# A state-space scan and a feed-forward network on one core: halves of a chunk's tokens, and another order and another engine for the lead-in's loads

## The chip, the cores and the metric

The kernel runs on one core of a Trainium2 chip. The core has five engines that each take their instructions in order: TensorE (PE in the profile; its weight loads are PEld), VectorE (DVE), ScalarE (ACT), GpSimd (POOL) and SyncE (SP). Data moves between DRAM and the core's memory through 16 DMA engines; SP and ACT can issue such transfers, each into a queue of its own. The metric is the time of one execution on the device in microseconds (us).

## The reference

Inputs are `x` (4 batches, 8 heads, 768 tokens, 32 channels), a decay `a` per batch, head and token, and `B` and `C` with 16 states per token. A linear recurrence runs over the tokens of each batch and head. In blocks of tokens it reads:

```python
la = log(clip(a)); cum = cumsum(la)             # within a block
M = (C @ B.T) * exp(cum[i] - cum[j]) * (i >= j)
y = M @ x + (C @ state) * exp(cum)
state = exp(sum(la)) * state + sum_j exp(cum[-1] - cum[j]) * B[j] x[j]
```

The outputs of the 8 heads of a token are put side by side to 256 numbers, and a feed-forward network follows for the 3072 tokens: `leaky_relu(y @ w_in, 0.01) @ w_out` with 2048 hidden features. All is float32 in the reference; the weights reach the kernel as 64-bit floats and are decoded on the chip.

## The kernel before, in words

The kernel takes 96 tokens to a chunk (8 chunks) and a chunk of one batch to a unit (32 units, `u = 4 * chunk + batch`). For each unit PE computes the score products (L288 or L365), DVE multiplies them with a tile of decays `lt` (L293 or L374), and `unit_products` multiplies the result with the tokens (L305) and the states' inputs `bn` with the same tokens (L314). The tile `xs` of a chunk holds the tokens of all 4 batches in its first 96 partitions and the states that enter the chunk in the last 16. `unit_halves` copies the new states on ACT (L336) and puts them on POOL into the next chunk's `xs` (L339), then takes the outputs as a high part `xh` (ACT, L341) and a low part `xl` (DVE, L344).

The decays of the first two units come directly from the logarithms (`reach`, L172, L215). Those of units 2 to 15 come from row sums of the logarithms: `split_sums` makes them on PE (L194) and splits them in three 16-bit parts on DVE (L195 to L198), which a DMA writes to DRAM (`parts_d`, L561), and two DMAs per group of units bring them back in another layout, into `dr` (L224) and `dl` (L227). One short matmul pair per unit (L234) then gives the exponents, and ACT the exp (L242). The first such pair of DMAs fetches the rows of units 2 to 5, later ones two units each.

The loop over units 0 to 15 is the lead-in. In it PE runs one unit's scores, the unit before's products and the decay of the unit after, DVE decodes the first weight blocks in steps (`decode`, L390 to L428), and `ps_d`, two PSUM buffers of two banks, holds in turn a unit's outputs and another unit's decay. `state_decay` (L269, POOL) scales a chunk's `bn` once it has landed.

Then the feed-forward network runs as 94 steps of one block of 128 features for 512 tokens: six matmuls in (L486), the leaky relu on ACT (L493, L496), the rest on DVE (L499), six matmuls out (L510). Units 16 to 31 are worked in between, two at a time.

The order of all instructions is written out by hand, and each engine keeps it (`manual_schedule`). Waits are put in from the data that instructions share. The loads come from helper functions (`fetch_w` L82, `fetch_bc` L86, `fetch_bn` L90, `fetch_x` L96) and before the change every DMA of the lead-in is issued by SP, so SP's order is: `la`, `bc` and `xs` of chunk 0, `parts_d`, `bn` of chunk 0, the first weight block, the rows `dr` and `dl`, and then `bc`, `bn`, `xs` of chunk 1, the second weight block and `xs` of chunk 2.

Of the kernel before, what the change touches and what calls it, by code (L numbers as in the profile page):

```python
# [10 lines left out]
F32 = mybir.dt.float32  # L11
# [6 lines left out]
NB, NH, S, D, N = 4, 8, 768, 32, 16  # L18
Q = 96
NC = S // Q  # L20
QE = Q + N
DM = NH * D
# [4 lines left out]
TS = 512  # L27
# [28 lines left out]
def scan_ffn(ctx: ExitStack, tc: tile.TileContext, a_l, bc_l, bn_l, x_l, w_l, out_l):  # L56
# [4 lines left out]
    wst = ctx.enter_context(tc.tile_pool(name="wst", bufs=3))  # L61
    wr = ctx.enter_context(tc.tile_pool(name="wr", bufs=RAWS))
    pbc = ctx.enter_context(tc.tile_pool(name="pbc", bufs=2))
    pxs = ctx.enter_context(tc.tile_pool(name="pxs", bufs=3))
    plt = ctx.enter_context(tc.tile_pool(name="plt", bufs=4))
    px = ctx.enter_context(tc.tile_pool(name="px", bufs=4))
    pg = ctx.enter_context(tc.tile_pool(name="pg", bufs=LAG + 1))
# [12 lines left out]
    def fetch_w(f, eng=nc.sync):  # L80
        raws[f] = wr.tile([128, 2 * DM, 2], U32, name="raw")
        eng.dma_start(raws[f].rearrange("p c w -> p (c w)"), w_l[f].bitcast(U32))  # L82

    def fetch_bc(c, eng=nc.sync):
        bcs[c] = pbc.tile([128, BC_COLS], F32, name="bc")
        eng.dma_start(bcs[c], bc_l[c])  # L86

    def fetch_bn(c):
        bns[c] = pbc.tile([QE, NB * NH * N + N], F32, name="bn")
        nc.sync.dma_start(bns[c], bn_l[c])  # L90

    def alloc_x(c):
        xss[c] = pxs.tile([QE, NB, DM], F32, name="xs")

    def fetch_x(c, eng=nc.sync):
        eng.dma_start(xss[c][:Q].rearrange("p b c -> p (b c)"), x_l[c])  # L96


    idle = const.tile([128, 512], BF16, name="idle")
# [13 lines left out]
    fetch_bc(0)  # L113
    for c in range(3):
        alloc_x(c)
    fetch_x(0)


    upto = const.tile([Q, QE], F32, name="upto")
# [97 lines left out]
                start=False, stop=True,  # L217
            )

    def decay_rows_of(u, n):  # L220
        p, b = u * NH, (u - DIRECT) % SLOTS
        r = Q + 3 * NH
        rows = parts_d[p:p + n * NH]
        nc.sync.dma_start(  # L224
            dr[r:r + 3, b:b + n].rearrange("i b h q -> i (b h) q"), rows.rearrange("p i q -> i p q")
        )
        nc.sync.dma_start(  # L227
            dl[Q:r, b:b + n, :Q], rows.rearrange("(b h) i q -> (h i) b q", h=NH)
        )

    def decay_pe(u, space):
        b = (u - DIRECT) % SLOTS
        for g in range(2):
            nc.tensor.matmul(  # L234
                heads_of(space, g), lhsT=dl[:KD, b], rhs=dr[:KD, b, 4 * g:4 * g + 4],
                start=True, stop=True,
            )
        decay_of(u, space)

    def decay_of(u, space):  # L240
        lt = lts[u] = plt.tile([QE, NH, Q], F32, name="lt")
        nc.scalar.activation(  # L242
            lt.rearrange("p (g h) i -> p g (h i)", g=2), space[:QE, :, :4 * Q], AF.Exp
        )
# [33 lines left out]
    def scores(u, warm=0):  # L278
        c, b = divmod(u, NB)
        spread = bcs[c][:, B_COLS:].rearrange("p (b i) -> p b i", b=NB)  # L280
        lt = lts[u].rearrange("p (g h) i -> p g (h i)", h=2)
        for half in range(2):
            sc = score_tile()
            if half == 0 and warm:
                keep_warm(sc[:, 0], warm)
            for g in range(2):
                r = 32 * (2 * half + g)
                nc.tensor.matmul(  # L288
                    sc[:QE, g, :2 * Q], lhsT=bcs[c][r:r + 32, b * QE:(b + 1) * QE],
                    rhs=spread[r:r + 32, b], start=True, stop=True,  # L290
                )
            heads = lt[:, 2 * half:2 * half + 2]
            nc.vector.tensor_tensor(out=heads, in0=sc[:QE, :, :2 * Q], in1=heads, op=ALU.mult)  # L293
# [3 lines left out]
    def unit_products(u, space, off=0):  # L297

        c, b = divmod(u, NB)
        kk = QE if c else Q  # L300
        mt, xs = lts[u], xss[c][:, b]
        for g in range(2):
            for hh in range(4):
                h = 4 * g + hh
                nc.tensor.matmul(  # L305
                    space[hh * D:(hh + 1) * D, g, off:off + Q],
                    lhsT=xs[:kk, h * D:(h + 1) * D], rhs=mt[:kk, h, :], start=True, stop=True,
                )
        if c + 1 < NC:

            for h in range(NH):
                hh = h % 4
                n0 = (b * NH + h) * N
                nc.tensor.matmul(  # L314
                    space[hh * D:(hh + 1) * D, h // 4, off + Q:off + Q + D],
                    lhsT=bns[c][:kk, n0:n0 + 2 * N],
                    rhs=xs[:kk, h * D:(h + 1) * D], start=True, stop=True,
                )

    def unit_halves(u, space, off=0):  # L320

        c, b = divmod(u, NB)
        yp = space[:, :, off:off + Q]
        pieces = []
        i = 0
        while i < Q:
            t, col = divmod(u * Q + i, TS)
            n = min(Q - i, TS - col)
            if col == 0:
                xh[t] = px.tile([128, 2, TS], F32R, name="xh")  # L330
                xl[t] = px.tile([128, 2, TS], F32R, name="xl")
            pieces.append((t, slice(col, col + n), slice(i, i + n)))
            i += n
        if c + 1 < NC:
            stage = pst.tile([128, 2, D], F32, name="stage")
            nc.scalar.copy(stage, space[:, :, off + Q:off + Q + D])  # L336
            to = xss[c + 1][Q:QE, b].rearrange("n (g h d) -> n g h d", g=2, d=D)
            for hh in range(4):
                nc.gpsimd.tensor_copy(to[:, :, hh], stage[hh * D:hh * D + N])  # L339
        for t, to, of in pieces:  # L340
            nc.scalar.copy(xh[t][:, :, to], yp[:, :, of])  # L341
        def rest():
            for t, to, of in pieces:
                nc.vector.tensor_tensor(  # L344
                    out=xl[t][:, :, to], in0=yp[:, :, of], in1=xh[t][:, :, to], op=ALU.subtract
                )
        return rest

    def unit_out(u, space):
        unit_products(u, space)  # L350
        return unit_halves(u, space)
# [183 lines left out]
                nc.sync.dma_start(out_l[m, :, t * TS:(t + 1) * TS], ob)  # L535


    with tc.tile_pool(name="ps_d", bufs=2, space=PSUM, reuse_waits="tile") as ps_d:

        def free_tile():  # L540
            return ps_d.tile([128, 2, TS], F32, name="pd")

        nc.vector.tensor_scalar(
            out=la, in0=la, scalar1=1e-6, scalar2=1.0, op0=ALU.max, op1=ALU.min,
        )
        nc.scalar.activation(la, la, AF.Ln)
        nc.vector.tensor_copy(dl[:Q], upto_b.unsqueeze(1).to_broadcast([Q, SLOTS, QE]))
        fill_later(0, 2)
        pds = [free_tile() for _ in range(DIRECT)]
        for u in range(DIRECT):  # L550
            fill_reach(u)
        for u in range(DIRECT):
            decay_mask(pds[u])
        split_sums(first[:, 0, :Q])
        fill_less(0, nc.scalar.copy)
        fill_less(1, nc.scalar.copy)
        second = score_tile()
        keep_warm(second[:, 1], WARM2)
        columns(erev, after, AF.Exp, second[:, 0])
        fill_later(2, SLOTS)  # L560
        nc.sync.dma_start(parts_d, parts)  # L561
        fetch_bn(0)
        fetch_w(0)
        decay_rows_of(DIRECT, SLOTS)
        fetch_bc(1)
        fetch_bn(1)
        fetch_x(1)
        fetch_w(1)
        fetch_x(2)
        decay_direct(0, pds[0])  # L570
        decay_of(0, pds[0])
        scores(0)
        state_decay(0)
        for b in range(2, SLOTS):
            fill_less(b, nc.gpsimd.tensor_copy)
        decay_direct(1, pds[1])
        decay_of(1, pds[1])
        decode_abs(0)
        for u in range(PE_DECAY):
            if u + 1 < PE_DECAY:  # L580
                scores(u + 1, 2 if u < 2 else 1)
            if u == 11:
                alloc_x(4)
            rest = unit_out(u, free_tile())
            v = u + 2
            if v < PE_DECAY:
                decay_pe(v, free_tile())
                if v % 2 and v + SLOTS <= PE_DECAY:
                    decay_rows_of(v + SLOTS - 1, 2)
            rest()  # L590
            if u > 2:
                settle()
            if u == 0:
                decode(2)
            elif u != 3:
                decode(1)
            if u == 2:
                state_decay(1)


            if u in (2, 6):
                fetch_bc(u // 4 + 2)
            if u in (3, 7):
                fetch_bn(u // 4 + 2)
                fetch_w(u // 4 + 2)
            if u == 3:
                alloc_x(3)
                fetch_x(3)
            if u in (6, 10):
                state_decay((u + 2) // 4)  # L610
        settle()
        decode(1)
# [100 lines left out]
```

## Time and profile before

| what | value |
|---|---|
| median of 3 runs | 330.37 us (328.43 to 330.88) |
| the profiled execution | 326.36 us |
| its span on the core | 324.7 us |
| granted TensorE clock | 1.00 |
| TensorE matmuls busy, instructions | 316.9 us, 2439 |
| VectorE busy, instructions | 160.3 us, 305 |
| ScalarE busy, instructions | 167.4 us, 334 |
| GpSimd busy, instructions | 80.5 us, 164 |
| DMA | 27.86 MB, mean 86 GB/s |

How the profile is read: it is one execution of the program, and all times in it run from the start of the span. A row of a timeline has the start in us, the length in us, the engine, the line of the kernel, the operation with the tile it writes and the tiles it reads, the shapes, the count, and in square brackets how long the engine sat idle before it and who released it. "SPq" and "ACTq" are DMA issues of SP and ACT. The chain of waits is followed back from the last instruction; "issue" in it is time in which an engine waited for nothing that the profile shows. A DMA row has its name, number, size and the median time from issue to landing. A queue's row has its packets, its MB and the time of its packets as a share of 16 engines.

### The profile page before, as it was taken

What the parts mean: (1) busy time and instruction counts of PE and PEld (TensorE: products, weight loads), DVE (VectorE), ACT (ScalarE), POOL (GpSimd) and SP (SyncE); (2) the same over time, 40 slices, a digit from 0 to 9 for tenths busy, and PEclk for the clock granted to TensorE, in tenths of its full rate; (3) what the DMA queues carried; (4) which work ended last, traced back from release to release, by engine and by line L of the source; (5) the groups of instructions that cost most, each with busy time, mean ns of one, the idle gap of its engine ahead of it and who ended that gap; (6) DMA issues with size and microseconds to landing.
All of it is one profiled execution on the core that took longest, in us unless ns stands there. A gap on an engine that the chain in (4) does not pass through costs nothing.

```text
span 324.7 us, 6255 instructions
## 1 busy us (share of the span) xinstructions
PE 316.9 (98%) x2439; PEld 250.4 (77%) x2440; DVE 160.3 (49%) x305; ACT 167.4 (52%) x334; POOL 80.5 (25%) x164
## 2 busy tenths in 40 slices
PE   8889999999999999999999999999999999999995
PEld 4456587888788877887788888888878788888883
DVE  5679978967688543524434342525252312322221
ACT  5567776674756545353454545453544444444431
POOL 3667820000010243454034543434210000000000
PEclk9999999999999999999999999999999999999999
DMA  5998032342891001602311090202010000100001
GB/s 159 311 312 249 30 118 73 129 131 78 281 297 32 1 0 67 203 9 74 107 23 65 0 280 27 87 2 86 2 65 2 0 0 2 63 3 0 3 0 65
DMA packets 10616, 27.86 MB, mean 86 GB/s; under 512 B 2170, under 2 KB 2650, under 8 KB 10586
## 3 DMA queue, kind: packets, MB, share of 16 engines
q1 hardware_dynamic: 10442, 27.33, 26.9%
q8 instruction: 19, 0.31, 0.4%
q10 hardware_dynamic: 144, 0.13, 0.1%
q14 instruction: 11, 0.09, 0.1%
HBM read 24.14 MB, written 3.32 MB: 85 GB/s over the span
## 4 chain that ended last, share of the span: by engine, by line
PE 95%; DMA 2%; DVE 1%; issue 1%; ACT 0%; SPq 0%; ACTq 0%
PE op L510 41%; PE hp L486 39%; PE sc L288 2%; PE pd L305 2%; PE sc L365 2%; PE sc L305 2%; PE pd L234 2%; PE sc L104 1%; DMA dl<-parts_d 1%; PE sc L486 1%; PE pd L314 1%; DMA parts_d<-parts 0%; PE sc L314 0%; PE pd L208 0%; DVE lt L293 0%
## 5 line engine op out<-in xcount | busy, mean ns | idle before, releaser
L499 DVE TENSOR_TENSOR gl<-hp,gh 128x512 fp32r<-128x512 f32 x94 | 65.0, 691 | 143.7 <-ACT hp L496 143.3
L493 ACT ACTIVATE gh<-hp 128x512 fp32r<-128x512 f32 x94 | 56.1, 597 | 110.6 <-PE hp L486 110.6
L510 PE MATMUL op<-gh,wh 128*128 128x512 f32 x192 | 76.3, 397 | 0.0
L510 PE MATMUL op<-gh,wl 128*128 128x512 f32 x192 | 74.8, 390 | 0.0
L510 PE MATMUL op<-gl,wh 128*128 128x512 f32 x192 | 74.8, 389 | 0.0
L486 PE MATMUL hp<-xh,wh 128*128 128x512 f32 x188 | 73.3, 390 | 0.0
L486 PE MATMUL hp<-xl,wh 128*128 128x512 f32 x188 | 73.2, 389 | 0.0
L486 PE MATMUL hp<-xh,wl 128*128 128x512 f32 x188 | 73.1, 389 | 0.0
L496 ACT ACTIVATE hp<-hp 128x512 f32<-128x512 f32 x94 | 55.7, 593 | 0.0
L510 PEld LDWEIGHTS op<-gh,wh 128*128 128x128 f32 x192 | 36.0, 188 | 10.5 <-issue 2.3
L510 PEld LDWEIGHTS op<-gl,wh 128*128 128x128 f32 x192 | 36.0, 188 | 7.6
L510 PEld LDWEIGHTS op<-gh,wl 128*128 128x128 f32 x192 | 36.1, 188 | 7.1
L339 POOL COPY xs<-stage 16x64 f32<-16x64 f32 x112 | 31.3, 280 | 39.7 <-ACT stage L336 29.6
L486 PEld LDWEIGHTS hp<-xh,wl 128*128 128x128 f32 x188 | 35.3, 188 | 7.4
L486 PEld LDWEIGHTS hp<-xh,wh 128*128 128x128 f32 x188 | 35.3, 188 | 7.4
L486 PEld LDWEIGHTS hp<-xl,wh 128*128 128x128 f32 x188 | 35.3, 188 | 7.3
L254 POOL TENSOR_TENSOR lt<-lt,ccol 112x768 f32<-112x768 f32 x16 | 23.5, 1469 | 50.5 <-DMA lt<-crow_d 49.4
L263 POOL TENSOR_SCALAR_AFFINE_SELECT lt<-lt 96x768 f32<-96x768 f32 x16 | 14.0, 875 | 59.5 <-ACT lt L262 59.5
L293 DVE TENSOR_TENSOR lt<-sc,lt 112x384 f32<-112x384 f32 x32 | 16.3, 549 | 3.1 <-ACT lt L242 1.9
L374 DVE TENSOR_TENSOR lt<-sc,lt 112x384 f32<-112x384 f32 x32 | 15.6, 549 | 0.5
L262 ACT ACTIVATE lt<-lt 112x768 f32<-112x768 f32 x16 | 13.4, 839 | 4.1 <-POOL lt L254 4.1
L242 ACT ACTIVATE lt<-pd 112x768 f32<-112x768 f32 x16 | 13.1, 816 | 2.1 <-PE pd L215 2.1
(89 smaller groups left out, 242.4 us busy)
## 6 DMA issues: line engine op xcount, KB each, us to landing
raw<-w_l SPq DMA_DIRECT2D x16, 512.0 KB, 3.4
lt<-crow_d SPq DMA_DIRECT2D x16, 336.0 KB, 4.7
bc<-bc_l SPq DMA_DIRECT2D x8, 608.0 KB, 5.8
xs<-x_l SPq DMA_DIRECT2D x8, 384.0 KB, 9.4
out_l<-ob SPq DMA_DIRECT2D x11, 256.0 KB, 2.8
bn<-bn_l SPq DMA_DIRECT2D x8, 231.0 KB, 5.7
out_l<-obh ACTq DMA_DIRECT2D x1, 128.0 KB
out_l<-obh SPq DMA_DIRECT2D x1, 128.0 KB, 1.8
```

The lines of the kernel that those rows point to most:

```text
L242: nc.scalar.activation(lt.rearrange("p (g h) i -> p g (h i)", g=2), space[:QE, :, :4 * Q], AF.Exp)
L254: nc.gpsimd.tensor_tensor(out=lts[u], in0=lts[u], in1=ccol[:, u * NH:(u + 1) * NH].unsqueeze(2).to_broadcast([QE, NH, Q]), op=ALU.subtract,)
L262: nc.scalar.activation(lt, lt, AF.Exp)
L263: nc.gpsimd.affine_select(out=lt[:Q], in_=lt[:Q], pattern=[[0, NH], [1, Q]], compare_op=ALU.is_ge, fill=0.0, base=0, channel_multiplier=-1,)
L293: nc.vector.tensor_tensor(out=heads, in0=sc[:QE, :, :2 * Q], in1=heads, op=ALU.mult)
L339: nc.gpsimd.tensor_copy(to[:, :, hh], stage[hh * D:hh * D + N])
L374: nc.vector.tensor_tensor(out=heads, in0=spaces[half][:QE, :, 2 * Q * e:2 * Q * (e + 1)], in1=heads, op=ALU.mult,)
L486: nc.tensor.matmul(hp, lhsT=w_half[half][:, f, k * 128:(k + 1) * 128], rhs=x[t][:, k, :], start=(n == 0), stop=(n == 5),)
L493: nc.scalar.activation(ghs[s], hp, AF.Prelu, alpha=0.01)
L496: nc.scalar.activation(hps[s], hps[s], AF.Prelu, alpha=0.01)
L499: nc.vector.tensor_tensor(out=gls[s], in0=hps.pop(s), in1=ghs[s], op=ALU.subtract)
L510: nc.tensor.matmul(op, lhsT=w_half[half][:, f, DM + m * 128:DM + (m + 1) * 128], rhs=x, start=(first and i == 0), stop=(last and i == 2),)
```

## The change

The tile `xs` of a chunk becomes two tiles of two batches each (the pool goes from 3 to 6 buffers of half the size), and `fetch_x` issues two DMAs. All loads of the start move to the front of SP's order: `la`, `bc` of chunk 0, the first weight block, `xs` and `bn` of chunk 0, `bc`, `bn` and `xs` of chunk 1, the second weight block and `xs` of chunk 2. The sums' write to `parts_d` and the first rows of `dr` and `dl` are issued by ScalarE, the rows behind unit 0's exp. The lead-in's outputs and decays get a PSUM pool each, of one buffer. `state_decay(1)` moves from unit 2 to unit 0.

```diff
-    pxs = ctx.enter_context(tc.tile_pool(name="pxs", bufs=3))
+    pxs = ctx.enter_context(tc.tile_pool(name="pxs", bufs=6))
...
     def alloc_x(c):
-        xss[c] = pxs.tile([QE, NB, DM], F32, name="xs")
+        for g in range(2):
+            xss[c, g] = pxs.tile([QE, NB // 2, DM], F32, name="xs")
 
     def fetch_x(c, eng=nc.sync):
-        eng.dma_start(xss[c][:Q].rearrange("p b c -> p (b c)"), x_l[c])
+        for g in range(2):
+            n = NB // 2 * DM
+            eng.dma_start(
+                xss[c, g][:Q].rearrange("p b c -> p (b c)"), x_l[c][:, g * n:(g + 1) * n]
+            )
...
     for c in range(3):
         alloc_x(c)
+    fetch_w(0)
     fetch_x(0)
+    fetch_bn(0)
+    fetch_bc(1)
+    fetch_bn(1)
+    fetch_x(1)
+    fetch_w(1)
+    fetch_x(2)
...
-    def decay_rows_of(u, n):
+    def decay_rows_of(u, n, eng=nc.sync):
...
-        nc.sync.dma_start(
+        eng.dma_start(
             dr[r:r + 3, b:b + n].rearrange("i b h q -> i (b h) q"), rows.rearrange("p i q -> i p q")
         )
-        nc.sync.dma_start(
+        eng.dma_start(
             dl[Q:r, b:b + n, :Q], rows.rearrange("(b h) i q -> (h i) b q", h=NH)
         )
...
-        mt, xs = lts[u], xss[c][:, b]
+        mt, xs = lts[u], xss[c, b // 2][:, b % 2]
...
-            to = xss[c + 1][Q:QE, b].rearrange("n (g h d) -> n g h d", g=2, d=D)
+            to = xss[c + 1, b // 2][Q:QE, b % 2].rearrange("n (g h d) -> n g h d", g=2, d=D)
...
-    with tc.tile_pool(name="ps_d", bufs=2, space=PSUM, reuse_waits="tile") as ps_d:
-
-        def free_tile():
-            return ps_d.tile([128, 2, TS], F32, name="pd")
+    with (
+        tc.tile_pool(name="ps_y", bufs=1, space=PSUM, reuse_waits="tile") as ps_y,
+        tc.tile_pool(name="ps_d", bufs=1, space=PSUM, reuse_waits="tile") as ps_d,
+    ):
+
+        def free_tile(of_outputs):
+            pool = ps_y if of_outputs else ps_d
+            return pool.tile([128, 2, TS], F32, name="py" if of_outputs else "pd")
...
-        pds = [free_tile() for _ in range(DIRECT)]
+        pds = [free_tile(u % 2 == 0) for u in range(DIRECT)]
...
-        nc.sync.dma_start(parts_d, parts)
-        fetch_bn(0)
-        fetch_w(0)
-        decay_rows_of(DIRECT, SLOTS)
-        fetch_bc(1)
-        fetch_bn(1)
-        fetch_x(1)
-        fetch_w(1)
-        fetch_x(2)
+
+        nc.scalar.dma_start(parts_d, parts)
         decay_direct(0, pds[0])
         decay_of(0, pds[0])
+        decay_rows_of(DIRECT, SLOTS, nc.scalar)
         scores(0)
         state_decay(0)
...
-            rest = unit_out(u, free_tile())
+            rest = unit_out(u, free_tile(u < PE_DECAY - 1))
             v = u + 2
             if v < PE_DECAY:
-                decay_pe(v, free_tile())
+                decay_pe(v, free_tile(False))
...
             if u == 0:
                 decode(2)
+                state_decay(1)
             elif u != 3:
                 decode(1)
-            if u == 2:
-                state_decay(1)
```

## The prediction

> **What bounds the kernel now.** I read the page first, then the chain that ended last, a table by stretches, and the four engines and the load queue through the first 24 us. The first row of the page, then the stretches (us; PE, PEld, DVE, ACT, POOL busy; clock; DMA share; GB/s):
>
> ```profile
> PE 316.9 (98%) x2439; PEld 250.4 (77%) x2440; DVE 160.3 (49%) x305; ACT 167.4 (52%) x334; POOL 80.5 (25%) x164
> ```
> ```profile
> 2.00:3.00 1.00, 1.00 (x4) 0.37 (x3) 0.79 (x4) 0.08 (x1) 0.70 (x4) 1.00 0.84 215
> 3.00:5.00 2.00, 2.00 (x8) 1.57 (x7) 0.95 (x4) 1.82 (x3) 1.36 (x2) 1.00 1.04 395
> 8.00:12.00 4.00, 3.07 (x48) 1.53 (x47) 1.93 (x4) 1.39 (x3) 2.35 (x3) 1.00 1.01 327
> 12.00:18.00 6.00, 5.86 (x132) 3.59 (x131) 5.53 (x13) 3.88 (x12) 4.70 (x14) 1.00 1.04 286
> 40.00:324.70 284.70, 280.83 (x1766) 228.79 (x1766) 129.50 (x227) 142.12 (x276) 54.06 (x91) 1.00 0.21 68
> ```
>
> PE carries the kernel. From 40 us on it is busy 280.8 of 284.7 us, with DMA at 0.21: no load edit reaches that stage. Everything the change can move lies in the lead-in, the first 40.8 us. There DMA is full (shares about 1.0) from 8 us on. The chain through it:
>
> ```profile
> 5.95 1.59 DMA parts_d<-parts
> ...
> 7.92 3.73 DMA dl<-parts_d
> ...
> 11.70 0.53 PE pd L234 x2
> ...
> 19.20 1.08 issue
> ...
> 40.83 2.94 PE hp L486 x12
> ```
>
> The split row sums make two trips through DRAM: out as `parts_d` (landed 7.54), back as rows of `dr` and `dl` (landed 11.65). The first decay made of them, unit 2's at L234, starts at 11.70; after that PE loses 1.08 us at 19.20 and little else. PE just before it:
>
> ```profile
> 10.70 0.33 PE L314 MATMUL pd<-xs,bn 96*32 96x32 f32 x16 [0.27 <-POOL bn L269]
> ```
>
> L314 ends at 11.03, so the rows cost PE 0.66 us; 0.27 us went to `bn`. What a perfect lead-in could give back here is 0.66 + 0.27 + 1.08 = 2.0 us, 0.6% of the time. A gain above 1% is almost excluded before the edits are read; a loss has no such ceiling, because PE stands behind L234 in order and each later microsecond of the rows is a microsecond of the kernel.
>
> **The change part by part.** Two edits have one answer: nothing. The PSUM pools: before, `free_tile` takes turns between two buffers, and the calls come as output, decay, output, decay, so all outputs up to unit 14 already have the first buffer and the decays the second; unit 15 has the second again. Own pools write the same down. That costs nothing. The halves of `xs`: L305 and L314 read one batch's columns, and state rows come from POOL by batch, so only the load's wait gets finer. It adds one issue per chunk, 0.42 us by the row at 1.72 below, on a queue that only waited from 2.1 to 5.95 before, and the halves' rows are 2 KB where they were 4 KB. `state_decay(1)` moves from unit 2 to unit 0, one POOL operation:
>
> ```profile
> 17.72 1.06 POOL L269 TENSOR_TENSOR bn<-bn,erev 112x512 f32<-112x512 f32 x1
> ```
>
> Its user is unit 4. Earlier, it has 1.06 us of POOL ahead of unit 1's state copies, which chunk 1 needs later still: zero while POOL waits for PE, 1.06 us if that cover were gone.
>
> What is left is the loads and the trip of the sums. SP's issues before, in order:
>
> ```profile
> 0.81 0.40 SPq L112 DMA_DIRECT2D la<-a_l  x1
> 1.26 0.41 SPq L86 DMA_DIRECT2D bc<-bc_l  x1
> 1.72 0.42 SPq L96 DMA_DIRECT2D xs<-x_l  x1
> 5.95 0.34 SPq L561 DMA_DIRECT2D parts_d<-parts  x1
> ...
> 10.10 0.66 SPq L96 DMA_DIRECT2D xs<-x_l  x1
> ...
> 20.05 0.36 SPq L82 DMA_DIRECT2D raw<-w_l  x1
> ```
> ```profile
> SPq L82 <- DMA xs<-x_l: 0.9, 1, 0.9
> ```
>
> The last row is the one that matters. The weight load at 20.05 waited 0.9 us for the landing of an `xs` load that it shares no buffer with. That `xs` load (10.10) is the 13th issue of the kernel, the weight load the 21st: eight apart. The program hands eight completion semaphores to its DMAs in turn, over all issuing engines, and the ninth must wait until the first has landed. Count the new order: la 1, bc0 2, w0 3, x0 4 and 5, bn0 6, bc1 7, bn1 8, x1 9 and 10, w1 11, x2 12 and 13, then from ScalarE `parts_d` 14, `dr` 15, `dl` 16. So `parts_d` waits until bn0 (6) is in, `dr` for bc1 (7), `dl` for bn1 (8). Before, nothing but DVE held `parts_d`. When is bn0 in? Sizes in the first 80 us (KB each, median us to landing):
>
> ```profile
> raw<-w_l SPq DMA_DIRECT2D x14, 512.0 KB, 3.4
> bc<-bc_l SPq DMA_DIRECT2D x4, 608.0 KB, 5.8
> xs<-x_l SPq DMA_DIRECT2D x4, 384.0 KB, 9.9
> bn<-bn_l SPq DMA_DIRECT2D x4, 231.0 KB, 3.7
> la<-a_l SPq DMA_DIRECT2D x1, 96.0 KB, 2.0
> ```
>
> The queue's sum up to bn0 is 96 + 608 + 512 + 384 + 231 = 1831 KB, up to bc1 2439, bn1 2670, and x2 3950. 215 GB/s put 210 KB in by 3.0 us; then 395 GB/s is 386 KB per us and 327 GB/s is 319. I take 350 between them, since the queue is full from the start and the engines get busy on the way. bn0's data is through at 3.0 + 1621/350 = 7.6, and I add 1.0 us for its completion (`parts_d` alone, 72 KB, took 1.59 from issue): 8.6, with 8.2 and 9.1 as ends. bc1 is in at 10.4, bn1 at 11.0, the whole queue drained at 13.7. ScalarE before:
>
> ```profile
> 5.76 0.38 ACT L190 ACTIVATE erev<-sc 112x256 f32<-112x256 f32 x1 [0.60 <-PE sc L189]
> 7.05 0.81 ACT L242 ACTIVATE lt<-pd 112x768 f32<-112x768 f32 x1 [0.91 <-PE pd L215]
> 9.05 0.81 ACT L242 ACTIVATE lt<-pd 112x768 f32<-112x768 f32 x1 [1.19 <-PE pd L215]
> ```
>
> The `parts_d` issue stands on ScalarE between the first two rows. While it waits, unit 0's exp (7.05) is queued behind it, and behind that exp DVE's product and PE's unit 0; unit 1's exp, the first weight pass and unit 0's output copies are queued behind the `dr` and `dl` issues. Issue at 8.6 instead of 5.95. Unit 0's exp then runs 9.0 to 9.8; before, L314 ended 3.2 us after that exp (7.86 to 11.03), so now at 13.0. This alone would put L234 at 13.0, +1.3 us.
>
> The trips: `parts_d` out alone costs 1.59, landing at 10.2. Beside a full queue its 128 rows of 576 B, eight per DMA engine, alternating with 4 KB rows at 350/16 = 22 KB per us, wait 8 x 0.19 = 1.5 us more: 11.7, which I take. Then `dr` and `dl` are issued, 0.36 apart as before, `dl` at 12.1. The nearest row for their landing is 3.73 us, behind bn0 and w0, 743 KB; at 11.7 the new queue still holds 3740 - 350 x 8.7 = 695 KB, about the same. That would land them at 15.8. On the other end stand 1.59 us, a small transfer served alone: with `parts_d` in at 10.2 and `dl` issued at bn1's 11.0, 12.6. I take 15.2, nearer to 3.73, because the backlog drains while they wait. L234 starts 3.5 us later than 11.70; ends +1.3 (unit 0's own chain) and +4.2.
>
> What is given back: the 1.08 us at 19.20. It is PE's code. PE's row, and the instruction queue:
>
> ```profile
> 20.29 0.37 PE L305 MATMUL pd<-lt,xs 112*32 112x96 f32 x7 [1.08 <-issue]
> ```
> ```profile
> q8 instruction: 19, 0.31, 0.4%
> ```
> ```profile
> q8 instruction: 1, 0.02, 14.8%
> ```
>
> The second row is the whole run's: 19 packets of 16 KB, for 2439 + 2440 = 4879 PE instructions, 257 to a packet. The third is the stretch 17.5 to 18.0, the only such packet in the first 22 us, taken while the load queue was full; PE stood mid-group until 20.29. With the queue drained at 13.7 and the next loads only at units 2 and 3, the packet comes in time: I take -1.08, bounds -1.08 and 0. DVE is nearly full in that stage too (5.53 of 6 us between 12 and 18), so some of it may not come through.
>
> Sum: 3.5 - 1.1 = +2.4 us; ends +1.3 - 1.1 = +0.2 and +4.2. The profiled execution took 326.36 us (span 324.7), below all three runs shown; its 326.4 + 2.4 = 328.8 stands for 330.4 + 2.4 = 332.8 in their median.
>
> **Rivals.** *Served at once, nothing waited for.* If ScalarE's queue neither waits nor shares, `parts_d` goes at 6.1 and lands at 7.7, the rows go behind the exp of 7.05 to 7.86 and land by 10.2; PE never waits, gains the 2.0 us, 328.4. The Trainium skill ("DMA: Bandwidth & Descriptors", Queues, rings and completion order) says that each DMA engine goes round between the queues that have work, packet by packet, so a small transfer in its own queue passes a backlog; by it alone the rows would come as in this rival. The late code packet speaks against it, the 20.05 wait more so: a transfer that isn't issued is in no queue. If the waits hold but service is prompt, it is the +0.2 end above. Chance 0.12, the prompt +0.2 case included.
>
> *Slower: the backlog first, on both trips.* If ScalarE's small rows get through only as the load queue drains, at 13.7, `parts_d` lands at about 14.7, the rows are issued by 15.4 and take 1.6 to 2.5 us: 17.0 to 17.9, L234 +5.3 to +6.2, less the 1.1 given back: 334.6 to 335.5. Without that gift, 336.6. It passes 1% once the rows land after 16.1 (11.70 + 3.3 + 1.1), only 0.3 us beyond the 15.8 above. For it: loads of the same kinds ran at 286 GB/s between 12 and 18 us, which moves every landing later. Against it: 395 GB/s early on. A slower clock could join, since PE would stand idle from 13.0 to 17: the first four warming matmuls, before any work,
>
> ```profile
> 1.26 1.89 PE sc L104 x4
> ...
> 14.24 0.27 PE sc L104
> ```
>
> took 0.47 us each in the chain, a later one 0.27; 1.89 us run at that pace instead loses 1.89 x (1 - 0.27/0.47) = 0.8 us, and the rival ends at 337.4 at most. The Trainium skill ("TensorE: Matmul & The Clock Gate", HAM oscillation) has the clock fall to half after an idle stretch of about 3.4 us; the granted clock stands at 1.00 in every stretch here, so no row shows it. Chance 0.37.
>
> **Numbers.** Within 1% (3.3 us, about what a measurement of this kernel can tell) 0.60: 0.48 for the forecast, 332.8 with its own 330.6 to 333.7, and 0.12 for the rival with the gain. Slower 0.37, faster 0.03 for what I don't see. The range, 328.6 to 336.4, runs from just inside the full gain to just inside the slow rival without the gift; what lies beyond is the cold clock and part of that gain.
>
> **What would show it.** ScalarE's `parts_d` issue near 8.6, waiting for bn's landing, not for DVE; `dl` issued near 12.1; L234 near 15.2; no idle mid-group near unit 4; the same length from the first hp matmul to the end. Wrong would be an issue at 6.1, or rows landed before 12.

## The result and the profile after

The changed kernel takes 333.0 us (median of six runs, 332.35 to 334.2), the kernel before 328.87 us beside it (six runs, 326.61 to 330.88). The ratio is 1.0122, interval 1.0076 to 1.0169: slower by about 1.2%. The profiled execution took 332.35 us, span 330.6, so 6.0 us more than the 326.36 of the one profiled before, itself below all six runs of its kernel. The medians differ by 4.1 us; the account below is that of the two profiled executions. Line numbers have moved: L234 is now L247, L305 L318, L314 L327, L242 L255, L561 L579, L224 and L227 L237 and L240, L486 L499.

The page, with TensorE's total and its granted clock in the 40 slices:

```profile
PE 318.8 (96%) x2440; PEld 251.5 (76%) x2440; DVE 161.2 (49%) x305; ACT 167.5 (51%) x334; POOL 80.3 (24%) x164
...
PEclk9669999999999999999999999999999999999998
```

The table by stretches (us; PE, PEld, DVE, ACT, POOL busy; clock; DMA share; GB/s):

```profile
8.00:12.00 4.00, 2.45 (x39) 1.26 (x41) 1.02 (x2) 0.81 (x1) 2.63 (x3) 0.92 1.05 324
12.00:18.00 6.00, 1.35 (x23) 0.74 (x16) 1.56 (x4) 1.91 (x5) 0.66 (x4) 0.50 0.48 152
18.00:22.00 4.00, 4.00 (x52) 2.10 (x51) 2.41 (x6) 1.63 (x4) 2.54 (x6) 0.55 0.02 4
```

The hole is between 12 and 18 us: PE was busy 5.86 of 6 us there before and now 1.35, and its clock stands at about half until 22. The chain of waits:

```profile
2.66 5.63 DMA xs<-x_l
...
8.37 6.33 DMA parts_d<-parts
...
15.25 1.67 DMA dl<-parts_d
...
16.96 0.89 PE pd L247 x2
...
46.76 2.99 PE hp L499 x12
```

The sums set out at 8.37 and landed at 14.70; the rows followed in 1.67 us. The first matmul into `hp`, with which the feed-forward network begins, came at 46.76 where it came at 40.83, 5.93 us later, and the whole span is 5.9 longer (330.6 for 324.7): all of the loss is in the lead-in. PE's timeline of the changed kernel:

```profile
10.21 0.59 PE L110 MATMUL sc<-idle 128*128 128x512 bf16 x2 [1.55 <-DVE lt L306]
...
11.86 0.45 PE L327 MATMUL py<-xs,bn 96*32 96x32 f32 x16
16.96 0.89 PE L247 MATMUL pd<-dr,dl 123*112 123x384 bf16 x2 [4.65 <-DMA dl<-parts_d]
...
20.57 0.89 PE L247 MATMUL pd<-dr,dl 123*112 123x384 bf16 x2
...
22.84 0.53 PE L247 MATMUL pd<-dr,dl 123*112 123x384 bf16 x2
```

and the same two later pairs before (the first one stood at 11.70):

```profile
13.71 0.53 PE L234 MATMUL pd<-dr,dl 123*112 123x384 bf16 x2
...
15.70 0.53 PE L234 MATMUL pd<-dr,dl 123*112 123x384 bf16 x2
```

Behind 4.65 us of idle the pair takes 0.89 us for 0.53, and two units last 22.84 - 16.96 = 5.88 us for 4.00: PE ran at a lower clock for two units. It didn't fall during that idle: the clock was already low while unit 0's products ran, when the longest idle so far had been the 1.55 us before 10.21:

```profile
11.40:12.30 0.90, 0.90 (x32) 0.78 (x28) 0.00 (x0) 0.00 (x0) 0.62 (x1) 0.50 1.10 294
```

ScalarE's queue, with its DMA issues:

```profile
8.37 0.34 ACTq L579 DMA_DIRECT2D parts_d<-parts  x1
8.76 0.81 ACT L255 ACTIVATE lt<-py 112x768 f32<-112x768 f32 x1 [2.96 <-PE pd L228]
...
14.72 0.49 ACTq L237 DMA_DIRECT2D dr<-parts_d  x1
15.25 0.30 ACTq L240 DMA_DIRECT2D dl<-parts_d  x1
```

What was the transfer doing in its 6.33 us? The queues, first over 8.37 to 12.7, then from 12.5 to 13.0, then from 13.0 to 13.5 (packets, MB, share; q1 is SP's queue, q10 ScalarE's):

```profile
q1 hardware_dynamic: 534, 1.37, 103.0%
```
```profile
q1 hardware_dynamic: 38, 0.16, 89.9%
q10 hardware_dynamic: 18, 0.01, 7.3%
```
```profile
q1 hardware_dynamic: 59, 0.15, 76.1%
q10 hardware_dynamic: 60, 0.03, 22.0%
```

For 4.3 us not one packet of `parts_d` moved, while 1.37 MB of loads issued earlier went by. Some 0.84 us of that is no wait for loads: in the kernel before, where no other packet moved, `parts_d` was issued at 5.95 and its first packet came at 6.79. Then both queues moved, at first packet for packet, 60 beside 59, and the 128 rows were through in 1.5 us. The Trainium skill ("DMA: Bandwidth & Descriptors", Queues, rings and completion order) has each DMA engine go round between queues packet by packet: these last rows agree, the 4.3 us before them do not, unless the packets had not yet reached the engines, which no run here shows.

The account of the 5.93 us. Rows: 16.96 - 11.70 = +5.26. From the first decay pair to the first hp matmul it is 46.76 - 16.96 = 29.80 now and 40.83 - 11.70 = 29.13 before. A run below that keeps the full clock shows 27.8 for the same stretch. So the clock costs about 2.0, and 1.3 is given back; 1.08 of it is the stall at 19.20, in which PE stood mid-group before and which is gone: 5.26 + 2.0 - 1.3 = 5.93.

### The profile page after: what moved, and what is told of

It reads as the page before. It is cut to its first block, busy times and chain, and to the rows that moved or that the text cites. A ratio compares the mean times of both kernels' runs of the same rounds, so it can differ in the third digit from the quotient of the medians.

```text
span 330.6 us, 6273 instructions
## 1 busy us (share of the span) xinstructions
PE 318.8 (96%) x2440; PEld 251.5 (76%) x2440; DVE 161.2 (49%) x305; ACT 167.5 (51%) x334; POOL 80.3 (24%) x164
## 4 chain that ended last, share of the span: by engine, by line
PE 92%; DMA 4%; ACT 1%; DVE 1%; SPq 1%; issue 0%; ACTq 0%
PE op L523 40%; PE hp L499 39%; PE sc L378 2%; PE sc L301 2%; PE sc L318 2%; DMA parts_d<-parts 2%; PE py L318 2%; PE pd L247 2%; DMA xs<-x_l 2%; PE sc L110 1%; PE sc L499 1%; PE py L327 1%; DMA dl<-parts_d 1%; PE sc L327 0%; ACT xh L354 0%
## 5 line engine op out<-in xcount | busy, mean ns | idle before, releaser
L499 PE MATMUL hp<-xh,wh 128*128 128x512 f32 x188 | 73.3, 390 | 0.0
L499 PE MATMUL hp<-xh,wl 128*128 128x512 f32 x188 | 73.3, 390 | 0.0
L499 PE MATMUL hp<-xl,wh 128*128 128x512 f32 x188 | 73.2, 389 | 0.0
L499 PEld LDWEIGHTS hp<-xh,wh 128*128 128x128 f32 x188 | 35.3, 188 | 7.4
L499 PEld LDWEIGHTS hp<-xh,wl 128*128 128x128 f32 x188 | 35.3, 188 | 7.4
L499 PEld LDWEIGHTS hp<-xl,wh 128*128 128x128 f32 x188 | 35.3, 188 | 7.4
L255 ACT ACTIVATE lt<-pd 112x768 f32<-112x768 f32 x15 | 12.2, 816 | 6.9 <-DMA dr<-parts_d 6.0
L275 ACT ACTIVATE lt<-lt 112x768 f32<-112x768 f32 x16 | 13.4, 839 | 4.1 <-POOL lt L267 4.1
```

The source lines that it names most:

```text
L275: nc.scalar.activation(lt, lt, AF.Exp)
L499: nc.tensor.matmul(hp, lhsT=w_half[half][:, f, k * 128:(k + 1) * 128], rhs=x[t][:, k, :], start=(n == 0), stop=(n == 5),)
```

## The experiments

The theory formed on this result is one of a backlog: a small transfer issued into another queue isn't served until the loads that the DMA engines already hold have gone by; SP's own wait for the sums used to keep these few. The rivals: the semaphore wait before the issue is the cause; ScalarE's queue is worse than SP's; the new tiles, PSUM pools or POOL's order cost time; the clock alone makes the loss. Ratios are to the kernel before in the same session; each kernel has line numbers of its own.

### The clock: more warming matmuls in the hole

```diff
-                scores(u + 1, 2 if u < 2 else 1)
+                scores(u + 1, 20 if u == 0 else 2 if u < 2 else 1)
```

18 matmuls are added whose result nothing uses.

> The changed kernel with 18 more warming matmuls of PE ahead of unit 1's scores (20 instead of 2), which fill PE's wait for the rows. If the clock's fall behind the 4.7 us wait costs time of its own: unit 2's decay matmuls start at 16.96 as in the changed kernel, the next such pair follows 2.0 us later instead of 3.6, the granted clock stays at 1.0, the first feed-forward matmul starts at about 45.0 instead of 46.8, and the time falls by 1.7 us (0.5%). If the clock in the records cost nothing and the slow pace there came from data or from other engines: the same 46.8 and the same time, or up to 0.3 us more.

332.81 us, 1.0183 (1.0097 to 1.0269). The chain and PE's timeline of this kernel:

```profile
8.83 7.22 DMA parts_d<-parts
```
```profile
18.25 0.53 PE L247 MATMUL pd<-dr,dl 123*112 123x384 bf16 x2 [1.98 <-DMA dl<-parts_d]
```

The pair takes 0.53 us again, the next follows 2.01 us later (20.26), and from 18.25 to the first hp matmul (46.04) it is 27.8 us: this is the stretch without a clock loss that the account above uses. `parts_d` took 7.2 us here, so the rows came 1.3 us later than in the changed kernel and the median hardly moved, where I had expected 1.7 us less. The clock is a part of the loss and not its cause.

### The same again, side by side with the changed kernel

> The changed kernel itself, on the same chip and beside the same runs of the kernel before as the next one, for the clock's share. Both theories: 1.0 to 1.7% over the kernel before, parts_d landing 5 to 7 us after its issue, granted clock at 0.5 between 12 and 18 us.

> The kernel with 18 more warming matmuls once more, now beside the changed kernel. In the first run of it the stretch from unit 2's decay to the first feed-forward matmul was 2.0 us shorter than in the changed kernel, but the rows had landed 1.3 us later, and the times didn't tell the two apart. If the clock's fall costs 2 us: the median is 1.5 to 2 us below the changed kernel's of the run above, and the stretch again 27.8 us against 29.8. If the rows land later because the warming matmuls are there (something that they hold up or disturb): again 1 us or more later than there, and no difference in the medians.

The changed kernel once more: 335.45 us, 1.0191 (1.0143 to 1.0239). With the warming: 332.05 us, 1.011 (1.0069 to 1.0151). PE's timeline of the changed kernel in this execution:

```profile
18.70 0.89 PE L247 MATMUL pd<-dr,dl 123*112 123x384 bf16 x2 [6.39 <-DMA dl<-parts_d]
...
22.31 0.89 PE L247 MATMUL pd<-dr,dl 123*112 123x384 bf16 x2
...
25.49 0.89 PE L247 MATMUL pd<-dr,dl 123*112 123x384 bf16 x2
```

and the chain with the warming:

```profile
18.09 0.53 PE pd L247 x2
...
45.89 2.95 PE hp L499 x12
```

The first pairs start at 18.70 and 18.09, but the first hp matmul came at 50.52 without the warming and at 45.89 with it. In the changed kernel the clock stayed low for three units, so that the stretch was 31.8 us: 4.0 of clock, for 2.0 in the first profile. The low clock lay elsewhere: it reads 1.00 up to 14.3, 0.50 from 14.4 to 28 and 1.00 again from there, while in the first profile it was low from about 11.4 and back at 22. Here `parts_d` took 7.57 us without the warming and 7.18 with it, so the warming matmuls are not what delays the rows. For the changed kernel I had expected 1.0 to 1.7%, `parts_d` in at most 7 us and a clock of 0.5 between 12 and 18 (0.70 measured), and missed all three by a little. The medians differ by 3.4 us in the direction expected, more than the 1.5 to 2 that I gave, because I had the clock's price from one execution. The warming doesn't repair the change: 1.1% stays (1.0183 in the first session, with overlapping intervals).

### The wait for the issue: whole tokens, one load

The halves of `xs` are undone (one tile, one DMA per chunk), which moves the count of the completion semaphores by one at chunk 0.

```diff
...
-        for g in range(2):
-            n = NB // 2 * DM
-            eng.dma_start(
-                xss[c, g][:Q].rearrange("p b c -> p (b c)"), x_l[c][:, g * n:(g + 1) * n]
-            )
+        eng.dma_start(xss[c][:Q].rearrange("p b c -> p (b c)"), x_l[c])
...
```

> The changed kernel with a chunk's tokens in one tile and one load again. There are three load issues fewer ahead of parts_d, so that its completion semaphore was last used by the first weight load and not by the second half of the tokens: parts_d can be issued at about 6.8 instead of 8.4, behind about the same 3.9 MB of loads. If small transfers wait until what was issued before them has gone through, whichever engine issued them: parts_d lands no earlier than before, at 14 to 15, the rows at 16 to 17, time as the changed kernel's within 0.5 us. If ScalarE's queue is served in turn with the load queue and the semaphores were what held it: parts_d lands 1.6 us earlier or more, the rows by 15.3, time 1.6 to 3 us shorter.

333.13 us, 1.0177 (1.011 to 1.0244). The chain, then the queues from 6.45 to 11.1:

```profile
6.45 8.64 DMA parts_d<-parts
```
```profile
q1 hardware_dynamic: 452, 1.32, 105.0%
```

The issue comes 1.9 us earlier, the landing (15.09) 0.4 us later than in the changed kernel. Again 1.32 MB passed before the first packet, and with more loads still queued it took 4 us more from there to the landing. The semaphore wait is real, but without 1.9 us of it the rows come no earlier, so it isn't the cause.

### Another issuing engine: the trip on SP behind the loads

```diff
-        nc.scalar.dma_start(parts_d, parts)
+        nc.sync.dma_start(parts_d, parts)
...
-        decay_rows_of(DIRECT, SLOTS, nc.scalar)
+        decay_rows_of(DIRECT, SLOTS)
```

> The changed kernel with parts_d and the first rows issued by SP behind all the front loads, instead of by ScalarE. If a small transfer waits until the 1.2 to 1.4 MB that the DMA engines already hold have gone by, in whichever queue it stands: parts_d, issued at about 9.9, lands with the last of the loads at 14.5 to 15.5, the rows at 17, time the changed kernel's within 1 us. If ScalarE's queue is served behind SP's as a rule: the trip lands 1 us earlier or more from SP although it is issued 1.5 us later, and the time falls by as much.

334.53 us, 1.0212 (1.0171 to 1.0253). The chain:

```profile
3.13 6.31 DMA bn<-bn_l
...
9.52 6.75 DMA parts_d<-parts
...
16.65 2.06 DMA dl<-parts_d
```

Behind the loads in the loads' own queue the trip takes 6.75 us, in a queue of its own 6.33. The second queue saved at most 0.4 us of it. The trip was issued 1.15 us later here (9.52, released by `bn`), and landed at 16.27 and the rows at 18.71, later than the 14.5 to 15.5 and the 17 that I had given.

### The queues exchanged

The kernel before, with the trip on SP as it was, but the loads that follow it (the first weight block, chunk 1's three, the second weight block, `xs` of chunk 2) on ScalarE; `bn` of chunk 0 goes ahead of the trip.

```diff
+    fetch_bn(0)
...
-        fetch_bn(0)
-        fetch_w(0)
         decay_rows_of(DIRECT, SLOTS)
-        fetch_bc(1)
-        fetch_bn(1)
-        fetch_x(1)
-        fetch_w(1)
-        fetch_x(2)
+        fetch_w(0, nc.scalar)
+        fetch_bc(1, nc.scalar)
+        fetch_bn(1, nc.scalar)
...
+        fetch_x(1, nc.scalar)
+        fetch_w(1, nc.scalar)
...
+        fetch_x(2, nc.scalar)
```

> The kernel before with the queues the other way round: SP has la, bc, tokens and bn of chunk 0 and then the sums' trip alone; the first weight block and all later loads of the start are issued by ScalarE, three behind the sums' exp (about 6.2 to 7.5), the others behind the exps of units 0 and 1. If SP's queue goes ahead of ScalarE's: the rows, issued at about 7.7, land by 10.2 with 2.6 MB of loads pending in the other queue, unit 2's decay starts at about 11. If both queues share as in the runs so far: the rows start when the 1.2 to 1.4 MB issued before them have gone by, 3.5 to 4 us after their issue, then go one by one between larger packets, and land at 14 to 18; time 2 to 6 us over the kernel before.

332.47 us, 1.0159 (1.0124 to 1.0194). The chain, then the queues from 9.82 to 13.4 (q10 now has the loads):

```profile
5.95 3.51 DMA parts_d<-parts
...
9.82 6.60 DMA dl<-parts_d
```
```profile
q10 hardware_dynamic: 390, 1.21, 102.5%
```

Now SP's small rows stand behind ScalarE's loads, for 3.6 us and 1.21 MB from `dl`'s issue until their first packet, in a queue that had already moved data. So it is neither ScalarE's queue nor the first use of a queue. The rows landed at 16.42, in the 14 to 18 that the backlog gave. `parts_d` itself shows the order of issue. It went out at 5.95, 0.3 us behind the first weight block and 0.1 us ahead of `bc` of chunk 1, and took 3.51 us for 1.59. ScalarE's queue from 5.95 to 8.45, just before its first packet:

```profile
q10 hardware_dynamic: 124, 0.51, 70.3%
```

That is 124 of the weight block's 128 rows, and nothing of the load issued after `parts_d`.

### Only the rows on ScalarE

The kernel before, with `parts_d` and all loads on SP in their old order, and only `dr` and `dl` issued by ScalarE.

```diff
-        decay_rows_of(DIRECT, SLOTS)
         fetch_bc(1)
...
         decay_of(0, pds[0])
+        decay_rows_of(DIRECT, SLOTS, nc.scalar)
```

> The kernel before with one edit: the first rows (dr and dl) are issued by ScalarE behind unit 0's exp, parts_d and all loads stay on SP in their order. SP then no longer waits for parts_d's landing before chunk 1's loads. If small transfers wait for what was issued before them: 608 KB and perhaps 231 KB more stand ahead of the rows than before, they land at 13.5 to 14.5 instead of 11.65, and the kernel is 1.5 to 3 us slower than before (more if the clock falls). If an own queue is served in turn: the rows land by 11, and the kernel is 0 to 0.7 us faster.

335.86 us, 1.0251 (1.0177 to 1.0324), the highest ratio of all, though its interval overlaps others. The chain, the queues from 8.16 to 11.0, and from 13 to 17.5:

```profile
8.16 9.61 DMA dl<-parts_d
```
```profile
q1 hardware_dynamic: 306, 1.08, 104.6%
```
```profile
q10 hardware_dynamic: 51, 0.01, 1.4%
```

On SP, between the loads, the same rows took 3.73 us; here 9.61. No load was moved, but as SP no longer waits for the sums' landing, `bc` of chunk 1 went out at 7.27 instead of 8.28, ahead of the rows. There is the wait at the start, and then a trickle: from 13 to 17.5 us only 51 small packets got through while the loads filled the engines. I had expected the rows at 13.5 to 14.5 and 1.5 to 3 us of loss; they landed at 17.77 and the median is 8.5 us above the kernel before's. One of the two edits, alone and in the kernel before, makes at least the whole loss: the chain's first `hp` matmul came at 47.55, against 46.76 in the changed kernel.

### A shorter queue

The changed kernel, with `xs` of chunk 1, the second weight block and `xs` of chunk 2 held back until unit 1.

```diff
-    fetch_x(1)
-    fetch_w(1)
-    fetch_x(2)
...
                     decay_rows_of(v + SLOTS - 1, 2)
+                if u == 1:
+                    fetch_x(1)
+                    fetch_w(1)
+                    fetch_x(2)
```

> The changed kernel with the loads behind chunk 1's bn (tokens of chunk 1, second weight block, tokens of chunk 2, 1.28 MB) held back until SP has issued the rows of units 6 and 7, and so with a queue of 2.67 MB instead of 3.95. parts_d's semaphore was last used by the first small load, so it is issued at about 6.1. If small transfers wait for what was issued before them: parts_d lands at about 11, when the 2.67 MB are through, the rows at 12.7, unit 2's decay at 12.8, 4.2 us earlier than in the changed kernel, no fall of the clock; time 5 us shorter than the changed kernel's, 0.5 to 1 us over the kernel before. If served in turn: parts_d lands at 8 to 9.5, the rows by 11.5, time at or below the kernel before.

332.94 us, 1.0167 (1.0118 to 1.0215). The chain, and PE's timeline:

```profile
6.18 5.43 DMA parts_d<-parts
...
12.16 1.77 DMA dl<-parts_d
...
22.08 8.47 DMA bc<-bc_l
...
30.56 5.09 DMA dl<-parts_d
```
```profile
13.98 0.89 PE L244 MATMUL pd<-dr,dl 123*112 123x384 bf16 x2 [3.06 <-DMA dl<-parts_d]
```

With fewer loads queued the rows come 3 us earlier, in the direction of the backlog and 1.2 us short of its 4.2. The time was a miss: I expected 5 us less and no fall of the clock, but the held loads now met the later ones (a `bc` at 22.08 took 8.47 us, and rows at 30.56 took 5.09), and the pair still ran slow after 3.06 us of idle, with the clock at 0.50 from 12.8 on, 1.9 us into it. The gain was given back to the next queue.

### Tiles, PSUM pools and POOL's order alone

The changed kernel with its trip and its loads put back as they were.

```diff
-    fetch_w(0)
     fetch_x(0)
-    fetch_bn(0)
-    fetch_bc(1)
-    fetch_bn(1)
-    fetch_x(1)
-    fetch_w(1)
-    fetch_x(2)
...
-        nc.scalar.dma_start(parts_d, parts)
+        nc.sync.dma_start(parts_d, parts)
+        fetch_bn(0)
+        fetch_w(0)
+        decay_rows_of(DIRECT, SLOTS)
+        fetch_bc(1)
+        fetch_bn(1)
+        fetch_x(1)
+        fetch_w(1)
+        fetch_x(2)
...
-        decay_rows_of(DIRECT, SLOTS, nc.scalar)
```

> The kernel before with three parts of the change and none of the moved DMAs: the tokens in halves, the two PSUM pools, state_decay(1) at unit 0. If the whole loss comes from the way of the sums: unit 2's decay starts at 11.7 and the time is the kernel before's within 0.5%. If the halves, the pools or the earlier state_decay cost something: their share of the 4 us shows here, with unit 2's decay at 11.7 all the same.

326.89 us beside 328.0: 0.9965 (0.9932 to 0.9997). The chain:

```profile
7.92 3.52 DMA dl<-parts_d
...
18.76 1.06 issue
...
25.48 1.60 issue
```

These parts cost nothing, and may gain a third of a percent, at the edge of what the runs can tell. The stretch from the first pair (11.48) to the first hp matmul (41.97) is 30.5 us, 27.8 without the two stalls.

### Can the lead-in be made shorter? Rows ahead of the weight block

The kernel before, with `bn` of chunk 0 ahead of the trip and the first weight block behind the rows.

```diff
     fetch_x(0)
+    fetch_bn(0)
...
-        fetch_bn(0)
-        fetch_w(0)
         decay_rows_of(DIRECT, SLOTS)
+        fetch_w(0)
```

> The kernel before with bn of chunk 0 moved to the front of SP's order (into the time in which SP waits for the sums) and the first weight block moved behind the rows, so that the rows find an empty queue. If it is the data issued ahead that delays the rows: they land at about 9.8 instead of 11.65, unit 2's decay starts behind unit 0's products at about 10.8, 0.9 us earlier, and the time is 0.3% shorter, less if the code packet comes late again. If the rows' landing has another cause: 11.6 as before and the same time.

328.28 us beside 328.0: 1.0021 (0.9994 to 1.0048). The chain, and PE's timeline:

```profile
8.42 3.46 DMA raw<-w_l
```
```profile
13.34 0.54 PE L306 MATMUL pd<-lt,xs 96*32 96x96 f32 x16 [0.78 <-DVE xl L345]
```

The first pair starts at 11.07, directly behind unit 0's products, so the rows' wait of 0.66 us is gone. But the weight block lands at 11.88, ScalarE's first weight pass stands in order ahead of unit 0's output copies, and PE now waits 0.78 us for those. A wait went and another came; the time didn't move, where I had expected a gain.

### The loads spread out

The kernel of the tiles alone, with `bn` of chunk 0 ahead of the trip, and the second weight block at unit 1, `xs` of chunk 2 at unit 3, the third weight block at unit 4, `xs` of chunk 3 at unit 5.

```diff
+    fetch_bn(0)
...
-        fetch_bn(0)
...
-        fetch_w(1)
-        fetch_x(2)
...
+            if u == 1:
+                fetch_w(1)
+            if u == 3:
+                fetch_x(2)
             if u in (3, 7):
                 fetch_bn(u // 4 + 2)
-                fetch_w(u // 4 + 2)
-            if u == 3:
+            if u in (4, 7):
+                fetch_w(u // 3 + 1)
+            if u == 5:
```

> The kernel of the tiles alone, with bn of chunk 0 at the front and fewer loads in flight: the second weight block is issued at unit 1, the tokens of chunk 2 at unit 3, the third weight block at unit 4 and the tokens of chunk 3 at unit 5. If PE's code packets come late because they too wait until the data that the DMA engines already hold has gone by: the two stalls in which PE waits for nothing the profile shows (1.06 and 1.60 us in the run of the tiles) shrink below 0.5 us each, the rows land by 11, and the time is 0.5 to 1% below the kernel before. If the packets are late for another reason: the stalls stay, and the time is that of the tiles, 0.3% below the kernel before, or no different from it.

326.84 us beside 327.78: 0.9976 (0.9943 to 1.001). The chain, and the instruction queue from 15.0 to 15.5:

```profile
7.93 3.10 DMA dl<-parts_d
...
18.98 0.27 issue
```
```profile
q8 instruction: 1, 0.02, 13.6%
```

The packet of the instruction queue that came between 17.5 and 18.0 in the kernel before, and between 17.0 and 17.5 in the tiles alone, comes here between 15.0 and 15.5, and both stalls of the tiles alone (1.06 and 1.60) are gone; the largest "issue" left in the chain of the lead-in is 0.27. The first hp matmul comes at 39.91, 0.9 us earlier than in the kernel before, but of the 0.5 to 1% that I expected the times show 0.24%, with 1.0 inside the interval. It isn't shown to beat the kernel before.

## Why the prediction was right or wrong

The time, 332.8, lies 0.2 us from the median and inside the range, but that is partly chance. The forecast was a difference of +2.4 us on a median of 330.4; measured are +4.1 on 328.9. The median I started from was 1.5 us too high and the difference 1.7 us too small, and the two cancel. I gave 0.60 to a time within 1% and 0.37 to slower by over 1%, and the latter came: the slower rival described the mechanism.

- **Where it can move.** Right: lead-in 5.93 us later, span 5.9 longer, nothing behind it. Halves, pools and `state_decay` at nothing: right, 0.9965 for the three together.
- **Issue of `parts_d` at 8.6, held by a completion semaphore.** Right in time (8.37) and in mechanism; the landing that released it was the second half of chunk 0's `xs`, not `bn0`, so my count was off by one. With the whole-tile load it was issued at 6.45 and landed no earlier: the step I worked out most closely didn't decide anything.
- **"Wait 8 x 0.19 = 1.5 us more: 11.7", the trip of `parts_d` at 3.1 us.** This is the step that failed. It took 6.33. The sharing was right, 1.5 us from 12.7 on; left out was what stands before it, 4.3 us in which 1.37 MB of earlier loads went by, against 0.84 us to the first packet of a transfer alone. I let the engines take turns from the moment of issue. The other steps that missed hang on this one: `dl` issued at 15.25 instead of 12.1, the first pair at 16.96 instead of 15.2.
- **The rows' landing 3.1 us after `dl`'s issue.** Too long: 1.67, since the load queue had drained by then. It made good a part of the miss above.
- **The stall given back, 1.08.** Right: PE doesn't stop mid-group there.
- **The clock.** Only the rival had it, at 0.8 us at most, from the pace of the first warming matmuls. It was 2.0 in the first profile and 4.0 in the second. The granted clock reads 0.50 and 0.55. The Trainium skill ("TensorE: Matmul & The Clock Gate", HAM oscillation) has it fall to half after some 3.4 us of idle. The half agrees, the length does not: the clock was at 0.50 from 11.40 in the first profile, ahead of the 4.65 us and behind 1.55 us of idle, from 14.4 in the second, 2.1 us into the 6.39, and in the run with the shorter queue 1.9 us into 3.06. With the warming, 1.98 us left it at 1.00. What sets the moment of the fall stays open.
- **The slower rival.** `parts_d` at 14.7, rows issued by 15.4, landed at 17.0, first pair +5.3: measured are 14.70, 15.25, 16.92 and +5.26. I gave it the smaller chance because of 395 GB/s early on, which bears on how fast a queue drains, and not on whether a second queue passes it. Its premise, that the small rows wait for the drain, is not quite what the runs show: with more loads queued, first packets moved while the loads still ran, after 1.2 to 1.4 MB, and the load queue was through at about 15.1, not at 13.7. So that its times fit to 0.2 us is partly chance too.

What stays open: whether that amount is set by bytes, by packets or by time, and where it is held. The runs show only how much went by. It isn't always so much: `parts_d` in the run with the queues exchanged waited for 0.51 MB, nearly all that ScalarE had issued before it, and in the run with the shorter queue it may have been simply all that was left.

## What to carry to other kernels

A small transfer with someone waiting for it should be issued before the bulk loads, or the bulk loads held until it is through; in these runs a queue of another engine didn't let it pass the first 1.2 to 1.4 MB of what had been issued already. A wait on the issuing engine can be a throttle that keeps a queue short, so look at what such a wait holds back before moving it. When waits on PE grow to some microseconds, add the slower clock behind them to the price; here it was 2 to 4 us.

## What the runs showed of the hardware

- Loads already issued go by first. Before the first packet of a small transfer in the other queue there passed 1.37 MB (changed kernel) and 1.32 MB (whole tokens), and for the rows, counted from the issue of `dr`, the first of the pair, 1.18 MB (only the rows on ScalarE, from 7.62) and 1.38 MB (queues exchanged, from 9.48). That took 3.4 to 4.7 us, for 0.84 us of a transfer alone, in either direction between SP and ScalarE. Packets of both queues move side by side only after that.
- A transfer of small rows can trickle beside a full queue: 51 packets in 4.5 us where ScalarE alone had the rows.
- The packets of the instruction queue, taken here for PE's code, share the DMA engines. Where the loads were spread the first came some 2 us earlier than in the tiles alone and the stalls of 1.06 and 1.60 us went; that the loads delayed it is argued from these times, not tried by itself.
- The length of the last idle stretch alone doesn't decide whether the granted clock falls: it read 0.50 behind 1.55 us of idle in the first profile of the changed kernel, and still 1.00 behind 1.98 us with the warming.
